# Other slots for x loads, one spectrum reload and two sequences' norms in a fused GFNet mixing and SwiGLU kernel

## The chip, the cores and the metric

The kernel runs on one core of one Trainium2 chip. The metric is the device time of one execution in microseconds (us), the median of the runs. Before the change it is 895.54 us, the median of three runs from 894.96 to 896.8 us.

## What is computed

There are 8 sequences of 3008 rows with 256 channels. Each goes through a Fourier filter along the sequence and then, row by row, through an RMS norm and a SwiGLU network of width 1536.

```python
X = np.fft.rfft(x, axis=1)                      # x: 8 x 3008 x 256
y = np.fft.irfft(X * (filt_r + 1j * filt_i)[None], n=3008, axis=1)
t = y.reshape(24064, 256)
xn = t / sqrt(mean(t * t, axis=-1) + 1e-6) * rms_g
g, v = xn @ w_gate, xn @ w_val                  # 256 x 1536
out = (g * sigmoid(g) * v) @ w_out              # 1536 x 256
```

## The kernel before

**Two kinds of work share the engines.** The heavy part is the network. Its items are `(b, m, jt)`: sequence `b` of 8, row group `m` of 6 (512 rows, or 384 in the last group of an even sequence), and one of 12 slices `jt` of the width. One item is called a *slot*, and the slots are counted from 0, 12 to a row group and 72 to a sequence. In a slot, `gv` (L506) makes the gate and the value with two matmuls each into `pg` and `pv`, ScalarE (ACT) applies Silu (`sg`, L510), VectorE (DVE) multiplies (`hh`, L511), and two slots later `down` (L523) adds `hh` times `wo` into `po` with four matmuls of 256 columns. After 12 slots `po` is copied to `o` and stored (`o_store`, L541).

**The Fourier filter of the later sequences is put between these slots as small steps.** For the sequence `b` they are, in order:

- `x_load` (L185): one of four transfers of 384 KB, from the input to an `xc` tile, issued by POOL (GpSimd). There are four `xc` buffers, and a load waits until the matmuls that read its buffer's old contents are done.
- `a_unit` (12 a sequence, three to an `xc` tile): one matmul `psa` (L205) and its copy; `z_store` (L210, SP queue) then writes a quarter of the result to memory.
- `t2_load` (L220, SP queue): the reload of that spectrum in another order, four transfers of 384 KB. It waits for all four `z_store`.
- `b_unit` (16 a sequence): four small matmuls `psb` (L240) and two multiplications with the filter on DVE (`s_part`, L230 and L233). `add_unit` (L267) is the sum on POOL. In the second sequence four of the 16 are `b_soft`, with ACT and POOL in the place of DVE.
- `yt_load` (L274, SP queue): a transposing transfer of the sums of two `b_unit`; `bi_unit` (L284) multiplies the result and copies it into `uu`; `t4_load` (L298, SP queue) transposes `uu` in four transfers.
- the norm, two halves for each row group: `n_unit` (L313, copy to `y`), `sq_unit` (L321, sums of squares on ACT), then `stat_unit` (L329, L331: factor `rho`) and `xt_unit` (L339: `xt` = `y` times `rho`) on POOL, then `tr_unit` (L348, SP queue): the transposing transfer `xn<-xt`. The first `gv` of row group `m` needs this `xn`.

**What sets the order.** Every engine and every queue works through its instructions in the order in which the program was written; SP and POOL don't wait for a slot, only for data and buffers, so they run ahead of the slots where nothing holds them. The order comes from a table `plan`: `at(slot, step)` enters a step, and the loop at L758 writes for each slot `gv`, then the entered steps, then `down`. `norm_plan` (L680), `a_plan` (L689) and `b_plan` (L704) choose the slots. Matmul steps go through `fit` (L661), which moves a step to the next slot in which its bank of PSUM is free and ACT and DVE are not too full. There is one bank `mx` for `psa`, `psi` and `psn`, and one bank `mb` for `psb`. `x_load`, `z_store`, `t2_load`, `t4_load`, `yt_load`, `stat_unit`, `xt_unit` and `tr_unit` aren't fitted; they follow at a fixed distance. Sequence 0 is worked through at the start, before slot 0, and its norms for the groups 2 to 5 are entered too.

Sequences are named by their index here: "x(2,0)" is the first x load of sequence 2, the third; "xn(1,0)" is the transposed norm of sequence 1, row group 0, which slot 72 needs.

Of the kernel before, what the change touches and what calls it, by code (L numbers as in the profile page):

```python
# [99 lines left out]
def kernel(  # L100
# [469 lines left out]
    with tc.manual_schedule():  # L570
# [83 lines left out]
        def at(slot, fn, *a):  # L654
            todo = (late if fn == q_unit else plan).setdefault(slot, [])
            if fn in front:
                todo.insert(0, (fn, a))
            else:
                todo.append((fn, a))

        def fit(slot, *need, keep=True):  # L661
            def fits(r, d, cost):
                i = slot + d
                if r in "MB":
                    return load[r][i] == 0
                wait = 0.0
                for k in range(max(0, i - 16), i + 16):
                    wait = max(0.0, wait + load[r][k] + (cost if k == i else 0.0) - room[r] - 0.15 * (k < 72))
                    if k >= i and wait > 0.6:
                        return False  # L670
                return True

            while not all(fits(*n) for n in need):
                slot += 1
            if keep:
                for r, d, cost in need:
                    load[r][slot + d] += cost
            return slot

        def norm_plan(b, m, slots, r):  # L680
            for i in range(2):
                s = fit(slots[i], ("M", 0, 1), ("A", 0, 0.6), ("A", 1, 0.82))
                at(s, n_unit, b, m, i)
                at(s + 1, sq_unit, b, m, i)
            for d, fn in zip(r, (stat_unit, xt_unit, tr_unit)):
                at(s + d, fn, b, m)
            assert s + r[-1] + 1 < 72 * b + 12 * m

        def a_plan(b, slots):  # L689
            for i in range(12):  # L690
                opts = []
                for k in "MB":
                    opts.append((k, "A", ((k, 0, 1), ("A", 0, 0.6))))
                    opts.append((k, "V", ((k, 0, 1), (k, 1, 1), ("V", 0, 0.68))))
                k, e, need = min(opts, key=lambda o: fit(slots[i], *o[2], keep=False))
                s = fit(slots[i], *need)
                at(s, a_unit, b, i, e, 0 if k == 'M' else 3)
                if i % 3 == 2:
                    at(s + 1, z_store, b, i // 3)
                    if b + 1 < B:  # L700
                        at(max(s + 2, {1: 19 + i // 3, 2: 62 + 2 * i}.get(b, 0)), x_load, b + 1, i // 3)
            return s + 1

        def b_plan(b, slots, lags, soft=()):  # L704
            for c in range(4):
                at(slots[0] - 4 + c if c < 3 else slots[4] + 1, t2_load, b, c)
            for i in range(16):
                if i in soft:
                    s0 = fit(slots[i], ("B", 0, 1), ("A", 0, 0.5))
                    at(s0, b_soft, b, i)  # L710
                else:
                    opts = [(k, ((k, 0, 1), (k, 1, 1), ("V", 0, 0.55), ("V", 1, 0.55)))
                            for k in ("BM" if b == 1 else "B")]
                    k, need = min(opts, key=lambda o: fit(slots[i], *o[1], keep=False))
                    s0 = fit(slots[i], *need)
                    at(s0, b_unit, b, i, 0 if k == "M" else 3)
                    at(s0 + 1, s_part, b, i, 1)
                    at(s0 + 2, add_unit, b, i)
                if i % 2:
                    at(s0 + 3 + (i in soft), yt_load, b, i // 2)  # L720
                    for u in (i - 1, i):
                        last = fit(s0 + lags[u % 2], ("M", 0, 1), ("A", 0, 0.49))
                        at(last, bi_unit, b, u)
            return last
# [10 lines left out]
        for b in range(1, B):  # L735
            t = (b - 1) * 72
            if b == 1:
                z = a_plan(b, [i for i in range(12)])
                b_at, lags = [z + 7 + 7 * i // 5 for i in range(16)], (9, 9)
                soft = range(2, 16, 4)  # L740
            elif b == 2:
                z = a_plan(b, [28 + 3 * i for i in range(12)])
                b_at, lags, soft = [z + 10 + 5 * i // 2 for i in range(16)], (8, 9), ()
            else:
                at_ = [72 + 3 * i if b == 3 else t - 87 + 4 * i for i in range(12)]
                z = a_plan(b, [s - (s % JT == 1) for s in at_])
                b_at, lags, soft = [t - 26 + 4 * i for i in range(16)], (8, 12), ()
            assert z + 3 <= b_at[0] - 4
            end = b_plan(b, b_at, lags, soft)
            for c in range(4):  # L750
                at(end + 1 + (3 * c if b < 3 else c), t4_load, b, c)
            n_at = end + 8 if b < 3 else t + 51
            assert n_at >= end + 4
            for m in range(6):
                norm_plan(b, m, (n_at + 8 * m, n_at + 8 * m + (4 if b > 1 else 2)), (2, 3, 7) if b > 1 else (2, 3, 6))
# [46 lines left out]
```

## Time and profile before

| what | value |
|---|---|
| median of 3 runs | 895.54 us |
| the profiled execution's own time | 894.35 us |
| its span in the trace | 892.6 us |
| granted TensorE clock, mean | 0.992 |
| PE (TensorE matmul) busy | 858.7 us, 96% |
| ACT busy | 614.8 us, 69% |
| DVE busy | 563.3 us, 63% |
| POOL busy | 297.9 us, 33% |
| slot 0 starts | 51 us |
| slot 24 (sequence 0, row group 2) starts | 93.87 us |
| slot 72 (sequence 1, row group 0) starts | 172.24 us |

Times in the trace count from the start of the span. "A <- B" in a list of waits means that A sat idle until B released it; three numbers follow: the sum in us, how often, and the longest. In the windows view a line has a stretch's bounds, its length, the busy time of PE, of PE's weight load, DVE, ACT and POOL with the number of their instructions, then the granted clock as a share of full speed, the busy share of the DMA engines (it can pass 1) and GB/s. In the list of DMA issues the last number is the median time in us from issue to landing, called the flight here.

### The profile page before, as it was taken

What the parts mean: (1) busy time and instruction counts of PE and PEld (TensorE: products, weight loads), DVE (VectorE), ACT (ScalarE), POOL (GpSimd) and SP (SyncE); (2) the same over time, 40 slices, a digit from 0 to 9 for tenths busy, and PEclk for the clock granted to TensorE, in tenths of its full rate; (3) what the DMA queues carried; (4) which work ended last, traced back from release to release, by engine and by line L of the source; (5) the groups of instructions that cost most, each with busy time, mean ns of one, the idle gap of its engine ahead of it and who ended that gap; (6) DMA issues with size and microseconds to landing.
All of it is one profiled execution on the core that took longest, in us unless ns stands there. A gap on an engine that the chain in (4) does not pass through costs nothing.

```text
span 892.6 us, 17021 instructions
## 1 busy us (share of the span) xinstructions
PE 858.7 (96%) x6134; PEld 533.2 (60%) x6134; DVE 563.3 (63%) x946; ACT 614.8 (69%) x1335; POOL 297.9 (33%) x342
## 2 busy tenths in 40 slices
PE   5899799699999999999999999999999999999997
PEld 4755466456566666666666666666666666665554
DVE  3955565377666666766666766766766666555554
ACT  4877477577768875788567875788657765677443
POOL 4813570345323440353214441344304440122100
PEclk9999899899999999999999999999999999999999
DMA  9967636887766556784666557564383333521101
GB/s 243 270 127 154 126 86 140 157 150 165 150 130 146 112 127 132 116 159 107 138 138 124 110 116 134 119 154 84 82 175 83 65 92 58 106 66 48 59 25 48
DMA packets 199205, 107.52 MB, mean 120 GB/s; under 512 B 159362, under 2 KB 183680, under 8 KB 199120
## 3 DMA queue, kind: packets, MB, share of 16 engines
q1 hardware_dynamic: 190608, 86.11, 44.3%
q0 software_dynamic: 8368, 20.19, 12.2%
q8 instruction: 48, 0.79, 0.4%
q14 instruction: 37, 0.30, 0.1%
q10 hardware_dynamic: 144, 0.13, 0.0%
HBM read 45.32 MB, written 35.65 MB: 91 GB/s over the span
## 4 chain that ended last, share of the span: by engine, by line
PE 87%; DMA 5%; DVE 2%; POOL 2%; ACT 2%; issue 1%; POOLq 0%; ACTq 0%; DVEq 0%
PE po L523 26%; PE pg L506 26%; PE pv L506 25%; DMA xn<-xt 3%; DMA xc<-in_x_dram 2%; PE psb L240 2%; PE psa L205 2%; PE psi L284 2%; PE psn L313 2%; DVE hh L511 1%; ACT sg L510 1%; DVE o L529 1%; POOL xt L339 0%; POOL ff L405 0%; PE psf L391 0%
## 5 line engine op out<-in xcount | busy, mean ns | idle before, releaser
L511 DVE TENSOR_TENSOR hh<-pv,sg 128x512 f16<-128x512 f32 (+2 forms) x578 | 392.1, 679 | 304.8 <-ACT sg L510 205.6
L510 ACT ACTIVATE sg<-pg 128x512 f16<-128x512 f32 (+2 forms) x578 | 338.0, 585 | 240.5 <-PE pg L506 236.5
L506 PE MATMUL pg<-xn,wg 128*128 128x512 f16 (+2 forms) x1156 | 338.8, 375 | 13.6 <-DMA xn<-xt 13.4
L523 PE MATMUL po<-wo,hh 128*128 128x256 f16 x2256 | 343.9, 273 | 1.9 <-DVE o L529 1.3
L506 PE MATMUL pv<-xn,wv 128*128 128x512 f16 (+2 forms) x1156 | 338.8, 375 | 0.0
L523 PEld LDWEIGHTS <-hh 128*128 128x128 f16 x2256 | 212.6, 98 | 115.2 <-issue 6.3
L506 PEld LDWEIGHTS <-wv 128*128 128x128 f16 x1156 | 113.3, 98 | 131.2 <-issue 1.3
L267 POOL TENSOR_TENSOR ss<-s,s 128x384 f16<-128x384 f16 x112 | 102.0, 911 | 268.2 <-DVE s L233 244.3
L506 PEld LDWEIGHTS <-wg 128*128 128x128 f16 x1156 | 112.9, 98 | 29.4 <-issue 8.4
L339 POOL TENSOR_TENSOR xt<-y,rho 128x1024 f16<-128x1024 f32 (+1 forms) x46 | 85.3, 1854 | 2.9
L321 ACT ACTIVATE junk<-y 128x256 f16<-128x256 f32 x180 | 74.2, 412 | 2.8
L233 DVE TENSOR_TENSOR s<-psb,ff 128x384 f16<-128x384 f32 x124 | 67.9, 548 | 0.0
L230 DVE TENSOR_TENSOR s<-psb,ff 128x384 f16<-128x384 f32 x124 | 67.9, 548 | 0.0
L194 ACT ACTIVATE uu<-psi 128x384 f16<-128x384 f32 x127 | 61.8, 487 | 1.0 <-PE psi L284 0.2
L194 ACT ACTIVATE y<-psn 128x512 f32<-128x512 f32 x96 | 56.3, 589 | 4.4
L329 POOL TENSOR_SCALAR u<-ss 128x4 f32<-128x4 f32 (+1 forms) x46 | 8.9, 193 | 132.1 <-ACT junk L321 131.8
L284 PEld LDWEIGHTS <-yt 96*128 96x128 f16 x512 | 35.3, 97 | 27.0 <-issue 1.0
L331 POOL TENSOR_TENSOR rho<-u,mhalf 128x4 f32<-128x4 f32 (+1 forms) x46 | 46.4, 1009 | 3.8
L284 PE MATMUL psi<-wi,yt 96*128 96x96 f16 x512 | 42.9, 205 | 0.1
L240 PE MATMUL psb<-wb,t 96*128 96x96 f16 x480 | 40.5, 207 | 2.0 <-DVE s L233 1.5
L194 ACT ACTIVATE t<-psa 128x512 f16<-128x512 f32 x66 | 38.9, 596 | 3.2 <-PE psa L205 1.8
L240 PEld LDWEIGHTS <-t 96*128 96x128 f16 x480 | 28.4, 98 | 13.9 <-DVE s L233 6.2
(82 smaller groups left out, 362.9 us busy)
## 6 DMA issues: line engine op xcount, KB each, us to landing
out_dram<-o SPq DMA_DIRECT2D x40, 512.0 KB, 3.3
xc<-in_x_dram POOLq DMA_DIRECT2D x31, 384.0 KB, 6.6
z_tmp<-t SPq DMA_DIRECT2D x28, 384.0 KB, 2.6
t<-z_tmp SPq DMA_DIRECT2D x28, 384.0 KB, 6.0
out_dram<-o SPq DMA_DIRECT2D x7, 384.0 KB, 2.7
ws<-in_moe_w_gate_dram POOLq DMA_DIRECT2D x3, 512.0 KB, 9.0
ws<-in_moe_w_val_dram POOLq DMA_DIRECT2D x3, 512.0 KB, 10.3
fs<-in_filt_i_dram POOLq DMA_DIRECT2D x2, 512.0 KB, 12.6
```

What stands on the lines that cost most here:

```text
L194: nc.scalar.activation(out=out, in_=in_, func=AXT.Copy, **({} if scale is None else {"scale": scale}))
L230: eng.tensor_tensor(out=o, in0=ps, in1=f1, op=ALU.mult)
L233: eng.tensor_tensor(out=o, in0=ps[:, :, ::-1, :], in1=f2, op=ALU.mult)
L240: nc.tensor.matmul(ps[:, ts(k, KR)], st[b]["t2"][kk // KC][:, kk % KC, ds(dh * P, P)], wb[:, kk, :], start=True, stop=True)
L267: nc.gpsimd.tensor_tensor(out=ss3[g % 3][:, :, dh, 0:KR], in0=s[0], in1=s[1], op=ALU.add)
L284: nc.tensor.matmul(ps[:, k, :], yt[0:KR, k, dh, :], wi[:, 4 * g + k, :], start=True, stop=True)
L321: nc.scalar.activation(out=junk, in_=y[:, i, ts(u, D)], func=AXT.Square, accum_out=ss[:, 2 * i + u:2 * i + u + 1])
L339: nc.gpsimd.tensor_tensor(out=xt[:, 0:n, :], in0=y.rearrange("p a (u d) -> p (a u) d", u=2)[:, 0:n, :], in1=rho[:, 0:n].unsqueeze(2).to_br ...
L506: nc.tensor.matmul(ps[:, 0:w], wt[:, dt_, ts(jt, P)], xn[:, q0:q1, dt_, :], start=(dt_ == 0), stop=(dt_ == 1))
L510: nc.scalar.activation(out=sg[:, c], in_=pg[:, 0:w], func=AXT.Silu)
L511: nc.vector.tensor_tensor(out=hh[:, c], in0=pv[:, 0:w], in1=sg[:, c], op=ALU.mult)
L523: nc.tensor.matmul(po[s4 // 2][:, s4 % 2, :], hh[:, ts(s4, P)], wo[:, jt, :], start=(jt == 0 and s4 % 2 == 0), stop=(jt == JT - 1 and (s4 ...
```

## The change

```diff
+        XAT = {2: (5, 8, 11, 29), 3: (47, 51, 79, 88), 4: (112, 122, 132, 142)}
+
         def a_plan(b, slots):
...
                     if b + 1 < B:
-                        at(max(s + 2, {1: 19 + i // 3, 2: 62 + 2 * i}.get(b, 0)), x_load, b + 1, i // 3)
+                        at(max(s + 2, XAT.get(b + 1, (0,) * 4)[i // 3]), x_load, b + 1, i // 3)
...
             elif b == 2:
                 z = a_plan(b, [28 + 3 * i for i in range(12)])
-                b_at, lags, soft = [z + 10 + 5 * i // 2 for i in range(16)], (8, 9), ()
+                b_at, lags, soft = [z + 13 + 7 * i // 3 for i in range(16)], (8, 9), ()
             else:
...
-                b_at, lags, soft = [t - 26 + 4 * i for i in range(16)], (8, 12), ()
+                b_at, lags, soft = [t - (25 if b == 3 else 26) + 4 * i for i in range(16)], (8, 12), ()
...
-            n_at = end + 8 if b < 3 else t + 51
+            n_at = end + (4, 6, 8)[b] if b < 3 else t + (53 if b == 3 else 51)
```

The slots in which the steps are entered follow from the code of the planner:

| step | slots before | slots after |
|---|---|---|
| x(2,0) to x(2,3) | 19, 20, 21, 22 | 6, 8, 11, 29 |
| x(3,0) to x(3,3) | 66, 72, 78, 84 | 47, 51, 79, 88 |
| x(4,0) to x(4,3) | 82, 93, 102, 111 | 112, 122, 132, 142 |
| norms of sequence 1, first `n_unit` to last `tr_unit` | 61 to 109 | 59 to 107 |
| `sq_unit`(1,0), second half; `tr_unit`(1,0) | 64; 69 | 62; 67 |
| `t2_load` of sequence 2 | 68, 69, 70, 83 | 71, 72, 73, 85 |
| `b_unit` of sequence 2, first to last | 72 to 109 | 75 to 110 |
| `t2_load`(3,0), first `b_unit` of sequence 3 | 114, 118 | 115, 119 |
| norms of sequences 2 and 3 | from 126; from 195 | from 127; from 197 |

On SP's queue xn(1,0) now stands ahead of all `t2_load` of sequence 2; before it stood behind the first of them. On POOL the first three x loads of sequence 2 stand ahead of the norm step of (0,2), where they stood behind it; x(3,0) and x(3,1) stand behind the norm step of (0,5) and ahead of that of (1,0). Several `a_unit` of the sequences 3 to 6 change their slot, or their copy changes from DVE to ACT or back. No step is added or removed.

## The prediction

> **What bounds the kernel now.** I read the page first: PE is busy for 96% of the span, and the chain that ended last is 87% PE. So only PE's idle time and its slow time can be won. Next I read the list of PE's waits; its four longest are these.
>
> ```profile
> PE pg L506 <- DMA xn<-xt: 13.4, 2, 6.7
> PE psa L356 <- DMA xc<-in_x_dram: 8.3, 2, 6.9
> PE psb L240 <- DVE s L233: 1.5, 1, 1.5
> PE po L523 <- DVE o L529: 1.3, 6, 0.3
> ```
>
> The reader is to see that beside the start (8.3 us, before slot 0) PE waits for one thing only: twice for a transposed norm. PE's timeline has the two places: 6.66 us before 93.87 (slot 24, xn(0,2)) and 6.74 us before 172.24 (slot 72, xn(1,0)). The windows view shows what comes with them.
>
> ```profile
> 88.00:90.00 2.00, 0.00 (x0) 0.00 (x0) 0.00 (x0) 0.00 (x0) 1.92 (x3) 0.97 1.08 204
> 90.00:92.00 2.00, 0.00 (x0) 0.00 (x0) 0.00 (x0) 0.00 (x0) 1.84 (x3) 0.50 1.13 210
> 94.00:96.00 2.00, 2.00 (x9) 0.93 (x8) 0.16 (x1) 0.60 (x1) 0.20 (x1) 0.50 1.16 206
> 96.00:98.00 2.00, 2.00 (x13) 1.25 (x11) 1.49 (x4) 0.61 (x2) 0.91 (x1) 0.83 0.00 0
> ```
>
> The eighth number is the granted clock: about 3 us after PE fell idle (87.2) it is halved, and it stays so until about 3 us of work are done. The DMA share above 1 says that the transfers were busy all through the wait. Then I read the DMA issues around the first wait, at 79.5 to 81.5 us, and for comparison those at 98 to 101 us and at 181.4 to 181.7 us.
>
> ```profile
> xc<-in_x_dram POOLq DMA_DIRECT2D x3, 384.0 KB, 9.8
> xn<-xt SPq DMA_TRANSPOSE x1, 14.2
> ```
>
> ```profile
> yt<-ss SPq DMA_TRANSPOSE x1, 3.0
> xn<-xt SPq DMA_TRANSPOSE x1, 3.9
> ```
>
> ```profile
> xc<-in_x_dram POOLq DMA_DIRECT2D x1, 384.0 KB, 5.2
> yt<-ss SPq DMA_TRANSPOSE x1, 6.0
> ```
>
> A transpose flies 3.0 to 3.9 us with no x load beside it, 6.0 us beside one, and 14.2 us beside four (the fourth is issued at 84.04 and lands, as the transpose does, at 93.83). At 162.3 there are two x loads beside xn(1,0), and it flies 9.8 us (162.41 to 172.20). In each case it lands 0 to 1 us after the last x load: 0.0, 0.3 and 0.9. The cause is plain in POOL's order: the end of `xt` releases SP's transpose and, as POOL's next instructions, the x loads (79.54 and 79.62; 162.33 and 162.41).
>
> **The x loads of sequence 2.** They go to slots 6, 8, 11 and 29. POOL is free after `rho` at 58.47 to 59.5, and the `a_unit` of the old contents are done in slots 4, 6 and 8 (56 to 64 us), so three loads start at about 59.5, 61 and 64 instead of 79.5 to 80.7. Cover: DMA share is 0 to 0.53 from 60 to 74. They lie beside four `z_store` (flight 2.3, the last issued at 69.75 and landed at 72.04). All three need 1.18 MB; at the some 200 GB/s of the rows above that is 6 us of the 15 us up to the first `t2_load` at 74.46, which waits for `o_store` at 73.55 in SP's order. So a `z_store` may land 2 us later at no cost. For xn(0,2), issued at 79.62 as before (its `xt` ends at 79.6), only the three `t2_load` are ahead.
>
> ```profile
> t<-z_tmp SPq DMA_DIRECT2D x3, 384.0 KB, 5.9
> ```
>
> The last is issued at 75.95 and lands at 82.51. The bounds for xn(0,2): 82.6 (flight 3.0) and 85.7 (flight 6.0, as beside one x load); I take 83.5, one us behind the last reload. PE needs it at 87.2. Margin 1.5 to 4.6 us: **the first wait goes, 6.66 us.** What is late next? The `yt_load` and `bi_unit` of sequence 1 now come some 8 us earlier, while POOL did work during the wait (1.92 and 1.84 of 2 us above). In POOL's order, with 0.91 us for an addition, 2.9 for a `b_soft` and 3.1 for a norm step, and the fourth x load's issue (0.6) in slot 29: xn(0,3) is issued at about 97 and needed at 105; the sums of b_unit 6 and 7 are done at about 101.5, their transpose, beside x(2,3), lands at about 107 at 6 us of flight, and `bi_unit` 6 is at about 108.5 in slot 38. This is the tightest; I take 0, at worst 1 us.
>
> **The norm of (1,0).** In the trace `sq_unit`(1,0), second half, is in slot 64, which starts at 157.09; `xt` ends at 162.38 and the transpose is issued at 162.41, 5.32 us after the slot's start. It moves to slot 62, at 154.46 plus 0.22 for the `psn` matmul that now comes earlier: issue at 154.68 + 5.32 = 160.0. Without the wait slot 72 would start where `po` ends: 165.01 + 3 x 0.109 = 165.34. So 5.3 us are there. No x load flies then (x(3,0) and x(3,1) start near 137, when xt(0,5) ends at 134.1 and the `a_unit` of slots 45 and 48 are done). Ahead in SP's queue is the last `t4_load`, landing at 162.10; a following transpose lands 1.2 us later at least (124.01 to 125.22, both of slot 39). So 163.1 to 163.9 (flight 3.1 to 3.9); beside a whole x load it would be 166.0. I take 163.5, **6.74 us gone**, with 0 to 0.7 us for the bound.
>
> **The clock.** Slots 24 and 25 took 98.00 - 93.87 = 4.13 us. Their work at full clock is eight matmuls at 0.216, eight of `down` at 0.109 and one `psb` step at 0.175: 2.78 us. Lost: 1.35. Slots 72 and 73 took 176.46 - 172.24 = 4.22 for 1.73 + 6 x 0.109 + 0.175 + 0.216 = 2.77. Lost: 1.45. These 2.80 us go with the waits; a remaining wait under 3 us would cost no clock, by the rows above.
>
> **Reloads of sequence 2** stand behind xn(1,0) on SP: issue at 161.3 or later, landing at 166.0 to 168 (flights 4.7 to 6.6) for the first. `b_unit` 0 is in slot 75 now, about 165.3 + 3.9 + 0.9 = 170.1. Cost 0, margin 2 us.
>
> **The rest.** x(3,2) and x(3,3) at slots 79 and 88 fly beside transposes (6 us) that have 5 slots or more (7.5 us) to their use. x(4,0) at slot 112 falls beside the transpose of sequence 2's last sums, as x(4,3) did at 237.49; the reload for `b_unit` 0 of sequence 3 landed there at 245.51 and was used at 246.13, 0.6 us in hand. Both move by a slot, but the last `z_store` ahead moves by two: 0 to 1 us, I take 0.3. On the other side PE had four gaps of 0.26 us before `psa` in slots 132, 144, 156 and 168 (trace 265.9 to 266.15 and on), each behind a `psi` one slot before in the same bank; these `a_unit` move two slots away: -1.0. Copies that go from DVE to ACT or back: 0, since both engines are below 70%. Sum: -6.66 - 6.74 - 2.80 - 1.0 + 0.3 = **-16.9 us**. The profiled execution's 894.35 becomes 877.4; it lies 1.2 under the median, so 895.54 becomes **878.6**.
>
> **A rule against this.** The row is above: one transpose beside four loads of another queue flies 14.2 us and not 3. The Trainium skill, page "DMA: Bandwidth & Descriptors", section "Queues, rings and completion order", says that each DMA engine takes turns between the queues, a packet at a time. By that a transpose should get about every second turn and land after at most double its lone time (an estimate, some 6 to 8 us), however many loads stand in the other queue; xn(0,2) would then have been held by the reloads of its own queue, which stay, and the sum would be 8.0 us smaller. Three cases in this trace go with the loads, so the rows decide.
>
> **Rivals.** (1) One wait stays: the transpose is held by its own queue (three reloads ahead of xn(0,2); `o_store` and `t4_load`, issued at 155.8 and 156.9, ahead of xn(1,0)). For it: xn(1,0)'s margin is only 1.4 to 2.2 us. Against: transposes with stores and transposes ahead fly 3.1 to 5.2. One wait whole with its clock is 8.1 us: **886.7**. (2) The change doesn't do what it says: POOL gets to the moved loads only when other transposes start, and waits of the same size come elsewhere: **895**. Against: the idle stretches of POOL at 59 to 76 and 134 to 144. (3) Slower: the `b_unit` of sequence 2 come every 7/3 slots, not 5/2, while `psb` has one bank that is free only after DVE's second `s_part`. The list of waits has one such wait of 1.5 us. If DVE lags so far that all 16 units wait 1.3 us, 20.8 us are lost: 878.6 + 20.8 = **899.4**; it decides from 1.1 us each on (16.9 / 16). Against: a unit needs 0.17 + 0.55 + 0.68 + 0.55 = 2 us of some 3.5 between units.
>
> **Chances.** Forecast 0.82, rival 1 0.10, rival 2 0.03, rival 3 0.05. The range takes in the bounds above: 878.6 + 0.7 + 1 + 0.7 and a part of rival 1 upward, and downward the 1.3 us of `po` waits and the 1.5 us of `psb` that may go too: 876 to 884. A measurement here can tell some 0.2% (1.8 us) from no change: faster 0.92, same 0.03, slower 0.05.
>
> **What would show it.** Right: PE's list of waits has no `xn<-xt` above 1 us; the clock stays at 1.00 from 60 us on; xn(0,2) flies under 6 us with no x load beside it; slot 24 starts near 87 and slot 72 near 157; the `psa` gaps at slots 132 to 168 are gone. Wrong: xn(0,2) lands after 87 without x loads (rival 1), x loads beside xn(1,0) (rival 2), `psb` waits on DVE of over 5 us between slots 75 and 110 (rival 3).

## The result and the profile after

The changed kernel takes 880.68 us (median of 4 runs, 879.99 to 880.95) against 895.25 us before (median of 4 runs, 893.02 to 896.8): a ratio of 0.9845 with a 95% interval of 0.982 to 0.987. That is 14.6 us less; 16.9 were forecast. The profiled execution took 880.92 us, its span is 879.1 us and its mean clock 1.0.

PE's list of waits after the change answers to the one shown of before; the lines between these are left out.

```profile
PE psa L356 <- DMA xc<-in_x_dram: 7.9, 2, 6.5
PE po L523 <- DVE o L529: 1.9, 8, 0.4
PE psb L240 <- DVE s L233: 1.8, 2, 1.5
...
PE psi L284 <- DMA yt<-ss: 0.3, 1, 0.3
PE psa L205 <- ACT uu L194: 0.2, 1, 0.2
```

The first line of before, 13.4 us for `xn<-xt`, is gone. At the bottom stand two kinds that were not there, and the waits for `o` went from 6 to 8. The windows view of the place where PE stood still, and the one transpose in the list of DMA issues from 79.5 to 81.5 us:

```profile
88.00:90.00 2.00, 2.00 (x17) 1.31 (x15) 1.76 (x4) 1.12 (x3) 1.92 (x3) 1.00 1.03 149
90.00:92.00 2.00, 1.72 (x13) 0.78 (x12) 2.00 (x4) 0.87 (x2) 1.84 (x3) 1.00 0.91 115
```

```profile
xn<-xt SPq DMA_TRANSPOSE x1, 3.7
```

PE works where it had stood, the clock stays at 1.00, and xn(0,2) flies 3.7 us instead of 14.2 (79.88 to 83.61). It is the only issue in this stretch: no x load flies with it, and the three reloads still stand ahead of it in its own queue.

**Where the time went and came back.** This table has the start of some slots in PE's timelines and the difference to the kernel before. The executions differ by up to 3.4 us before slot 0 already (it starts at 49.5 to 52.9 us in the traces of this study), so a difference is read against the one at slot 0. It is taken from the starts before rounding.

| slot | before | after | difference |
|---|---|---|---|
| 0 | 50.77 | 50.66 | -0.11 |
| 23 | 85.29 | 85.18 | -0.11 |
| 26 | 98.00 | 89.70 | -8.31 |
| 71 | 164.15 | 156.38 | -7.77 |
| 74 | 176.46 | 159.95 | -16.50 |
| 119 | 246.74 | 229.20 | -17.54 |
| 180 | 337.03 | 321.94 | -15.09 |
| 252 | 437.80 | 424.41 | -13.40 |
| 575 | 885.10 | 871.67 | -13.43 |

The gain is made in two steps, at slots 24 and 72, and reaches 17.5 us at slot 119. Then 4.1 us are given back up to slot 252, and nothing happens after that. Of these 4.1 us, 3.8 are idle time of PE; the other 0.35 us is work, one `psb` and one `psi` step that moved from before slot 119 to behind it.

### The profile page after: what moved, and what is told of

It is laid out like the page before. It is cut to its first block, busy times and chain, and to the rows that moved or that the text cites. A ratio compares the mean times of both kernels' runs of the same rounds, so it can differ in the third digit from the quotient of the medians.

```text
span 879.1 us, 17015 instructions
## 1 busy us (share of the span) xinstructions
PE 857.4 (98%) x6134; PEld 532.0 (61%) x6134; DVE 559.5 (64%) x941; ACT 614.5 (70%) x1340; POOL 297.1 (34%) x342
## 4 chain that ended last, share of the span: by engine, by line
PE 87%; DMA 4%; DVE 3%; ACT 3%; issue 2%; POOL 0%; POOLq 0%; DVEq 0%; ACTq 0%
PE po L523 26%; PE pg L506 26%; PE pv L506 25%; PE psn L313 2%; PE psa L205 2%; PE psb L240 2%; DMA xc<-in_x_dram 2%; PE psi L284 2%; ACT sg L510 2%; DVE hh L511 2%; DVE o L529 1%; DMA ws<-in_moe_w_gate_dram 1%; DMA yt<-ss 1%; ACT junk L321 0%; PE psf L391 0%
## 5 line engine op out<-in xcount | busy, mean ns | idle before, releaser
L194 ACT ACTIVATE t<-psa 128x512 f16<-128x512 f32 x71 | 42.1, 596 | 3.5 <-PE psa L205 1.9
```

The lines of the kernel that those rows point to most:

```text
L194: nc.scalar.activation(out=out, in_=in_, func=AXT.Copy, **({} if scale is None else {"scale": scale}))
```

## Experiments

**The theory**: the x loads on POOL's queue hold the transposes that fly beside them; moving these loads is the whole gain, and the 4.1 us come from the other edits, through PE's bank of PSUM and ACT. **The rivals**: the transposes are held by their own queue, or the norms' earlier slots carry the gain.

**x2_only.** The kernel before with one edit:

```diff
-    at(max(s + 2, {1: 19 + i // 3, 2: 62 + 2 * i}.get(b, 0)), x_load, b + 1, i // 3)
+    at(max(s + 2, {1: (5, 8, 11, 29)[i // 3], 2: 62 + 2 * i}.get(b, 0)), x_load, b + 1, i // 3)
```

> The kernel before with the four x loads of sequence 2 alone in their new slots (6, 8, 11, 29). Theory (the x loads of the other queue hold the transpose): xn(0,2) flies under 5 us, the wait before slot 24 and its slow clock go (8.0 us), the wait before slot 72 stays at 6.7 us: 887.2 us. Rival (the three reloads ahead in the transpose's own queue hold it): xn(0,2) still lands after 87 us, no gain, 895 us.

Measured: 886.87 us, ratio 0.9913 (0.9889 to 0.9937). From slot 23 to slot 26 the trace gains 8.19 us; xn(0,2) flies 3.72 us behind the same three reloads. The wait before slot 72 stays (5.5 us in this execution, with two x loads beside a transpose that flies 8.6 us). The rival of the own queue falls as the cause of the wait; that queue still counts in the 3.7 us, since in the changed kernel its last reload landed at 82.84 and xn(0,2) at 83.61.

**x34_only.** As x2_only, but with the loads of sequences 3 and 4 alone:

```diff
+    at(max(s + 2, {1: 19 + i // 3, 2: (47, 51, 79, 88)[i // 3],
+                   3: (112, 122, 132, 142)[i // 3]}.get(b, 0)), x_load, b + 1, i // 3)
```

> The kernel before with the x loads of sequences 3 and 4 alone in their new slots. Norms and reload of the others stay. Theory: the wait before slot 24 stays; xn(1,0) is issued as before, some 2.9 us ahead of its need, and lands 3.2 to 4.2 us after issue, so 0.3 to 1.3 us of the wait before slot 72 stay and no slow clock: gain 6.9 to 7.9 us, 887.3 to 888.4 us. Rival (the earlier slots of the norms carry the second wait's end): at least half of the 6.7 us wait stays, 891 us or more.

Measured: 887.52 us, ratio 0.9918 (0.9895 to 0.9941). The first line of PE's waits is now

```profile
PE pg L506 <- DMA xn<-xt: 10.0, 1, 10.0
```

that is, one wait, the first, which in this execution, the longest of the ten (891.04 us), lasted 10.0 us. Of the second only 0.3 us is left, though the norms stand where they stood: xn(1,0) flies 3.12 us and lands at 170.28, slot 72 starts at 170.33, and slots 71 to 73 take 8.06 us less than before. So the earlier norms are worth no more than this 0.3 us of it.

**x_all.** Both edits together, and nothing else of the change (`{1: (5, 8, 11, 29), 2: (47, 51, 79, 88), 3: (112, 122, 132, 142)}`).

> The kernel before with all x loads in their new slots and nothing else of the change. Theory: both waits go but for 0.3 to 1.3 us, and nothing is given back between slots 119 and 252, where the changed kernel loses 4.1 us: 879 to 880.5 us, no slower than the changed kernel (880.7). Rival (the norms and the reload are needed for the gain): 884 us or more.

Measured: 878.1 us, ratio 0.9821 (0.9773 to 0.987), a little less than the 879 to 880.5 us expected. PE's waits have no `xn<-xt` left (before slot 72 PE loses 0.3 us, in which its weight load waits for xn(1,0)):

```profile
PE psa L356 <- DMA xc<-in_x_dram: 7.9, 2, 6.6
PE psb L240 <- DVE s L233: 1.8, 2, 1.5
PE po L523 <- DVE o L529: 1.3, 6, 0.3
```

The waits for `o` are 6 again, as before the change. Against the kernel before, the trace gains 8.19 us from slot 23 to 26 and 8.03 from 71 to 74, and from slot 119 to the end the difference stays at -17.2, of which -1.15 stood at slot 0 already. Counted from slot 0, x_all gains 16.1 us and the changed kernel 13.3. Moving the x loads alone is thus more than the whole gain; on balance the other edits take 2.8 us of it away, before slot 119 gaining some and behind it losing more.

**no_x.** The changed kernel with the x loads in the slots of before (the `x_load` line put back).

> The changed kernel with the x loads in the slots of before: norms and reload moved alone. Theory: the wait before slot 24 stays whole; xn(1,0) is issued 2.4 us earlier but two x loads start with it and it flies 9.8 us again, so some 4.3 us of the second wait stay; with the 4.1 us given back after slot 119 the sum is near zero: 893.5 to 896 us. Rival (moving the norms ends the second wait): 890 us.

Measured: 890.08 us, ratio 0.9947 (0.9927 to 0.9968). This expectation failed, and the rival's 890 us was met, though not by its mechanism as stated. The issues around xn(1,0), from 157 to 158.5 us, are

```profile
xc<-in_x_dram POOLq DMA_DIRECT2D x1, 384.0 KB, 5.6
xn<-xt SPq DMA_TRANSPOSE x1, 6.5
```

One x load, not two: with the norms two slots earlier, the step of (1,1) stands ahead of x(3,1) in POOL's order and holds it back until 166.5 us. With one load the transpose flies 6.5 us, and the second wait shrinks to 0.8 us (PE waited 4.8 us in two waits, the longer 4.0). The first wait, 4.0 us, was shorter than the 6.7 us of before too, though nothing up to slot 24 was moved; this execution was the shortest of the ten (887.89 us). So the norms' move is a second way to end most of that wait, through POOL's order; beside moved x loads it has the 0.3 us of above left to gain.

**beside1, beside2, beside3.** The changed kernel with one, two or three x loads of sequence 2 put back beside xn(0,2): `XAT[2]` is (5, 8, 19, 29), (5, 19, 20, 29) and (19, 20, 21, 29).

> The changed kernel with one x load, x(2,2), put back beside xn(0,2) (slot 19). Theory (a transpose waits for every x load that flies beside it): xn(0,2) lands 0 to 1 us after that load, flight 5.5 to 7 us against 3.7 with none; it lands at 85.5 to 87 us, PE waits 0 to 0.3 us. Rival (the queues take turns): flight 4 to 6 us.

> As beside1 with two x loads, x(2,1) and x(2,2), beside xn(0,2). Theory: flight 9 to 10.5 us, landing with the second load near 89 to 90; PE waits 2 to 3.2 us before slot 24 and, as the wait is under 3 us, the clock stays at full speed: slots 24 and 25 take 2.8 us. Rival (the queues take turns, a transpose needs at most double its lone time): flight 6 to 8 us, wait under 1 us.

> As beside1 with three x loads beside xn(0,2), at slots 19 to 21 as in the kernel before, the fourth at slot 29. Theory: flight 11 to 13 us, wait 4 to 6 us, the clock is halved after about 3 us of it and slots 24 and 25 take 3.5 to 4.2 us: 4.5 to 7 us more than the changed kernel. Rival: flight no longer than in beside2.

Measured in one execution each: 881.62, 882.18 and 887.42 us. The DMA issues at the transpose, for one, two and three loads:

```profile
xc<-in_x_dram POOLq DMA_DIRECT2D x1, 384.0 KB, 5.1
xn<-xt SPq DMA_TRANSPOSE x1, 6.0
```

```profile
xc<-in_x_dram POOLq DMA_DIRECT2D x2, 384.0 KB, 7.0
xn<-xt SPq DMA_TRANSPOSE x1, 9.8
```

```profile
xc<-in_x_dram POOLq DMA_DIRECT2D x3, 384.0 KB, 9.2
xn<-xt SPq DMA_TRANSPOSE x1, 12.0
```

With none it was 3.7, so each load adds 2.2 to 3.8 us, and the transpose lands 0.98, 0.30 and 0.00 us after the last load. The rival's flights, about double the lone time (6 to 8 us) with any number of loads, are not met.

The packets of the transfers show why. First comes one microsecond of the kernel before, 82.5 to 83.5 us, in which xn(0,2) and the x loads alone are under way; then half a microsecond of the changed kernel, 82.5 to 83 us, with xn(0,2) alone. A queue's line has packets, MB and the share of the 16 DMA engines' time; q0 has the x loads of POOL, q1 the transfers of SP.

```profile
DMA packets 115, 0.19 MB, mean 187 GB/s; under 512 B 59, under 2 KB 59, under 8 KB 115
q0 software_dynamic: 56, 0.17, 94.6%
q1 hardware_dynamic: 59, 0.02, 11.4%
```

```profile
q1 hardware_dynamic: 462, 0.12, 104.2%
```

Side by side the two queues' packets go one for one, 56 against 59 (in beside3 61 against 60 from 82 to 83 us). But a packet of an x load has 3072 bytes and took 270 ns of an engine (94.6% of 16 us, by 56); one of the transpose has 256 bytes and took 31 ns. So the transpose moved 59 packets in a microsecond beside a load, and 462 in half of one alone. In the traces xn is 1024 packets and an x load 128, so one load after another gets through while most of the transpose is still to come. By these numbers a load costs it about 128 x (270 + 31) / 16 ns = 2.4 us (an estimate); 2.2 to 3.8 were measured. It need not outlast every load: in the breaks between two loads it catches up, and in no_x xn(0,2) landed at 90.72, 0.44 us before the third load and 2.5 us before the fourth.

PE waits 0, 2.3 and 4.4 us. The windows view shows the clock, of beside2 first and then of beside3:

```profile
86.00:88.00 2.00, 0.00 (x0) 0.00 (x0) 0.46 (x1) 0.59 (x3) 1.33 (x2) 1.00 0.95 182
88.00:90.00 2.00, 1.76 (x14) 1.12 (x14) 0.51 (x1) 0.60 (x1) 1.76 (x4) 1.00 0.78 196
```

```profile
88.00:90.00 2.00, 0.00 (x0) 0.00 (x0) 0.00 (x0) 0.00 (x0) 1.92 (x3) 0.74 1.16 204
90.00:92.00 2.00, 0.77 (x2) 0.25 (x2) 0.00 (x0) 0.00 (x0) 1.76 (x4) 0.50 1.20 228
92.00:94.00 2.00, 2.00 (x11) 1.20 (x10) 0.80 (x2) 0.60 (x1) 1.79 (x1) 0.50 0.65 109
94.00:96.00 2.00, 2.00 (x9) 0.80 (x7) 0.82 (x2) 0.60 (x1) 0.91 (x1) 0.56 0.00 0
```

After a wait of 2.3 us the eighth number is 1.00 and slots 24 and 25 take 2.77 us. After 4.4 us it is 0.50 and they take 4.98 us. The expectation's 3.5 to 4.2 was too little: the clock stayed low until about 95.8 us (0.56 in the last line).

**a4_n51.** The changed kernel, to find what gave 4.1 us back:

```diff
-                at_ = [72 + 3 * i if b == 3 else t - 87 + 4 * i for i in range(12)]
+                at_ = [72 + 3 * i if b == 3 else t - (86 if b == 4 else 87) + 4 * i for i in range(12)]
...
-            n_at = end + (4, 6, 8)[b] if b < 3 else t + (53 if b == 3 else 51)
+            n_at = end + (4, 6, 8)[b] if b < 3 else t + (51 if b == 3 else 51)
```

> The changed kernel with two slots mended: the steps of sequence 4's x transform start one slot later, so that none stands one slot behind a psi whose copy waits for the sums of squares, and the norms of sequence 3 start at t + 51 as in the kernel before. Theory (what is given back after slot 119 are PE's waits for the one bank mx behind a copy that ACT does late): 2.3 to 2.9 us less than the changed kernel, about 878.1 us, the gaps before psa at slots 137 to 165 gone, the three gaps of 0.33 us in po after slots 146, 158 and 170 still there. Rival (the time is given back by DVE's later multiplications of sequence 3 alone): no more than 0.5 us less.

Measured: 877.81 us (877.41 to 882.03), ratio 0.981 (0.9787 to 0.9833), about 2.9 us less than the changed kernel. The run makes both edits at once, so it doesn't say which of them ends which gap. First the gap in the changed kernel, slot 137, in PE's and ACT's timelines (start, length, line, operation; the bracket is idle time):

```profile
256.17 0.59 PE L506 MATMUL pv<-xn,wv 128*128 128x512 f16 x2
256.85 0.38 PE L205 MATMUL psa<-xc,wa 128*128 128x512 f16 x1
```

```profile
255.38 0.41 ACT L321 ACTIVATE junk<-y 128x256 f16<-128x256 f32 x1
255.69 0.19 ACT L321 ACTIVATION_READ_ACCUMULATOR junk<-y 128x1 f32 x1
255.92 0.42 ACT L321 ACTIVATE junk<-y 128x256 f16<-128x256 f32 x1
256.24 0.18 ACT L321 ACTIVATION_READ_ACCUMULATOR junk<-y 128x1 f32 x1
256.33 0.47 ACT L194 ACTIVATE uu<-psi 128x384 f16<-128x384 f32 x1
256.70 0.58 ACT L510 ACTIVATE sg<-pg 128x512 f16<-128x512 f32 x1
```

Two matmuls of 0.216 us after 256.17 make 256.60; `psa` starts at 256.85. It uses the bank `mx` of the `psi` one slot before (255.12), whose copy into `uu` runs from 256.33 to 256.80, behind the sums of squares (`junk`, 1 us) of the same slot. In a4_n51 the same place reads

```profile
256.22 0.59 PE L506 MATMUL pv<-xn,wv 128*128 128x512 f16 x2
256.65 0.60 PE L523 MATMUL po<-wo,hh 128*128 128x256 f16 x4
```

and `psa` comes a slot later (257.95), without a gap. From slot 119 to 180 the changed kernel gives back 2.45 us against before and a4_n51 0.93 (0.35 us of each is the work that moved past slot 119); from 180 to 252 it is 1.69 against 0. As expected, three gaps of 0.33 us in `po`, after slots 146, 158 and 170, stay: in slots 144, 156 and 168 the sums of squares and a `psi` copy still fall together, just ahead of the copy of `po`. The changed kernel's DVE timeline has the link at slot 145: DVE waits for ACT's `sg`, so its multiplication, and the copy of `po` behind it, come late.

```profile
269.78 0.69 DVE L511 TENSOR_TENSOR hh<-pv,sg 128x512 f16<-128x512 f32 x1 [0.65 <-ACT sg L510]
270.39 0.68 DVE L529 COPY o<-po 128x512 f32<-128x512 f32 x1
```

**seq3_late.** The changed kernel with `t - 22` in the place of `t - 25` and `t + 56` in the place of `t + 53` for sequence 3.

> The changed kernel with the spectral steps of sequence 3 and its norms three slots later still (t - 22 and t + 56 in the place of t - 25 and t + 53). The second multiplication on DVE then no longer stands in a slot before the copy of po, and no psa of sequence 4 one slot behind a delayed copy. Theory (what is given back after slot 119 are waits for the bank mx and for the copy of po): both kinds of gap go between slots 119 and 252, 3.5 to 4.5 us less than the changed kernel, 876 to 877.5 us; up to 1 us of it may be lost at slot 202, where the copies into uu come near the landing of t4. Rival (the time is given back by the later reload and norms of sequence 3 as such): slower than the changed kernel, 882 us.

Measured: 876.45 us (876.0 to 876.7), ratio 0.98 (0.9779 to 0.9821): the lowest median of all. Both kinds of gap are gone between slots 119 and 202; the difference to before goes from -17.81 at slot 119 to -18.87 at slot 180. In slot 203 `psa` is late by 0.69 us:

```profile
351.01 0.49 ACT L194 ACTIVATE uu<-psi 128x384 f16<-128x384 f32 x1 [1.30 <-PE pg L506]
```

ACT sat idle for 1.3 us although `pg` was long done; the last `t4_load`, which reads `uu`, landed at 350.86. Moving sequence 3 still later would run further into this.

**x_all_b.** x_all with `z + 10 + 7 * i // 3` for sequence 2 and `t + 52` for the norms of sequence 3.

> The kernel before with all x loads moved (as in x_all, 878.1 us) and two small shifts: the units of sequence 2 every 7/3 slots from the same start, the norms of sequence 3 one slot later. Theory: the four gaps of 0.26 us before psa and some waits for po between slots 84 and 204 go: 1 to 1.6 us less than x_all, 876.5 to 877 us. Rival (denser units make psb wait for DVE): 879 us or more.

Measured: 877.74 us, ratio 0.9813 (0.9792 to 0.9835). The expectation failed. The `psa` gaps did go, but PE's waits show a new line:

```profile
PE psi L284 <- DMA yt<-ss: 0.6, 2, 0.3
```

In slots 178 and 250 a `yt` transpose flew 7.3 and 6.0 us beside an x load and came 0.5 us late each time. Counted from slot 0, x_all_b had gained 17.45 us at slot 240 and 16.8 at 252; x_all has 16.1 in both. So 0.7 us of the 1 to 1.6 expected is left, and about 1 us went to the same mechanism that the change was about.

## Why the prediction was right, and where its sizes were off

- **The two waits and the clock** (-6.66, -6.74, -2.80, sum 16.20). Confirmed in mechanism and size: in x_all, where nothing else moves, the two places give 8.19 + 8.03 = 16.22 us. That the two sums agree to 0.02 is luck: both are read against the same trace of before, and in other executions with the x loads unmoved the first wait was 4.0 and 10.0 us and the second 5.5. Before slots 24 and 72 the half clock came with the waits of 4.0 us and more and not with that of 2.3 (beside2). The prediction's "a remaining wait under 3 us would cost no clock" doesn't hold as a rule: in beside3 the clock was halved 2.2 us after PE fell idle (idle from 86.80; 0.74 over 88 to 90 us puts the change at 88.96), and in beside1 it was 0.50 from 30 to 32 us, behind a wait of 1.5 us (26.39 to 27.92).
- **x loads hold the transpose, not its own queue.** Confirmed by x2_only, x34_only and the beside series: flights go 3.7, 6.0, 9.8, 12.0 with the number of loads. Rival 1 and rival 2 fall.
- **"A rule against this" was no rule against it.** The Trainium skill ("DMA: Bandwidth & Descriptors", section "Queues, rings and completion order") says that each DMA engine takes turns between the queues, a packet at a time, and the traces agree: 56 packets against 59 in the microsecond above. What failed is my estimate from it, double the lone time at most. It took a turn of either queue to be equally long, where the load's took 270 ns and the transpose's 31. The prediction came out right because it went by the rows; why they were so it had not understood.
- **Cover of the early x loads.** The loads started at 59.3, 61.0 and 64.7; two `z_store` beside them flew 6.6 and 6.2 us instead of 2.3, so they landed about 4 us later, twice what I had allowed, but the last landed at 72.86, ahead of the first reload at 74.35. No cost, as forecast.
- **Tight places.** xn(1,0) was issued at 151.87 and landed at 155.07, 2.3 us ahead of slot 72 (157.36); the first reload of sequence 2 landed at 158.10, well ahead of slot 75 at 161.32. The "tightest" place, `bi_unit` 6, cost nothing.
- **The norms of sequence 1** were credited with part of the second wait's end. They were hardly needed: x34_only ends all but 0.3 us of it without them.
- **The term that was mis-sized** is "four gaps of 0.26 us before psa ... these `a_unit` move two slots away: -1.0", with +0.3 for the rest. I followed the four that were there and didn't look for new pairs. The shift made six new gaps of 0.25 us (slots 137, 141, 149, 153, 161, 165), gaps in `po` of 0.2 to 0.45 us in slots 122, 134, 146, 158, 170 and 182, and four of 0.2 to 0.5 us at 210, 211, 215 and 250: with the four old ones gone and some smaller ones come, PE idles 3.8 us more between slots 119 and 252 where I had -0.7. Before slot 119 the other edits brought 0.9 us of idle time less that I hadn't counted; the two errors partly cancel. "Copies that go from DVE to ACT or back: 0, since both engines are below 70%" gives a reason that doesn't hold: an average says nothing about one slot in which ACT has two extra steps. What those copies themselves cost, no run separates.
- **The size of the sum by the medians.** The traces differ by 13.4 us, the medians by 14.6: the profiled execution of before was one of the shorter. Over 22 runs the kernel before took 890.46 to 898.54 us, the changed one over 4 runs 879.99 to 880.95. The waits themselves varied (the first one 6.7 us in the trace of before, 10.0 in x34_only and 4.0 in no_x, whose schedules up to slot 24 are the same), so part of the scatter is likely theirs.
- **Rival 3** (DVE holds `psb`) fell: `psb` waits went from 1.5 to 1.8 us.

Open: the packet counts explain why the flights go with the loads, but no run changed the size of a packet. Whether x loads in smaller packets, or a transpose in larger ones, would shorten the flight is not shown, and neither is why the same crowd of four loads gave flights of 11.5, 14.2 and 17.5 us (no_x, before, x34_only).

## What to carry to other kernels

Look at what a releasing step sets free besides the transfer that is needed: here the end of one POOL step started a transpose and three loads within 1.2 us, with a fourth 4.4 us after the transpose, and the one that PE waited for landed last, with the fourth load. Move loads that aren't urgent to stretches in which the queues are empty, and check every transpose that they then fly beside for its distance to use (here 6 us for one load, 10 for two, 12 for three). When two queues share the DMA engines, compare their packets and not only their bytes: here a transfer in 256-byte packets had one turn for each 3072-byte packet of the other. When steps are shifted in a full schedule, count the pairs that come to stand in the same or the next slot, not only the ones that go: a sum of squares and a copy in one slot cost 0.2 to 0.45 us each time, 2.1 us more idle time in the five row groups from slot 119 to 180.

## What the runs showed that I had not expected

- A copy that waits for the sums of squares of its own slot delays PE in the next slot even though ACT is busy for about 70% of the span only.
- Moving a load can be undone by in-order queues in either direction: in no_x, POOL's order alone kept one of two loads away from the transpose and cut the second wait from 6.7 to 0.8 us.
- The half clock isn't tied to the wait's length. After 4.4 us of waiting in beside3, slots 24 and 25 lost 2.2 us; after 4.0 us in no_x 2.5; after 6.7 us in the kernel before 1.35. By the windows the half clock lasted 6.8 us in all three (96:98 at 0.83 in the kernel before puts its end at 96.7), 10.2 in x34_only and 3.4 in x2_only, multiples of 3.4 us, and in these five it began between 2.2 us (beside3, no_x) and 5.0 us (x2_only) after PE fell idle. What is lost comes to about half of the time by which it outlasts the wait (beside3: 95.8 less 91.23, 4.6 us). In x2_only PE was idle from 159.54 to 165.05:

```profile
162.00:164.00 2.00, 0.00 (x0) 0.00 (x0) 0.00 (x0) 0.00 (x0) 0.00 (x0) 1.00 1.07 217
164.00:166.00 2.00, 0.95 (x3) 0.40 (x4) 0.00 (x0) 0.00 (x0) 0.00 (x0) 0.64 1.24 203
166.00:168.00 2.00, 2.00 (x11) 1.10 (x10) 0.95 (x2) 1.50 (x5) 0.19 (x1) 0.50 0.92 159
168.00:170.00 2.00, 2.00 (x12) 0.98 (x10) 1.10 (x3) 1.48 (x3) 1.90 (x2) 1.00 0.00 0
```
